# Windowed attention with routed experts on one core: value products round the column tiles, smaller value loads, split exps, and a planner that counts transfers

## The chip, the cores and the metric

The kernel runs on 1 core of one Trainium2 chip. The metric is device time in microseconds (us) of one execution, over several runs. The profile is of one more execution, whose own time is given beside its span (first to last recorded instruction).

## The reference, cut to what matters

Eight sequences of 576 tokens go through attention with 8 heads of 64. Heads 0 to 3 ("plain") see the last 32 positions, heads 4 to 7 ("dilated") the last 32 positions at distance 4. The result, as 512 features a token, goes through a mixture-of-experts step in which the 128 best-scored tokens of each sequence get a two-layer network added.

```python
scores = scale * np.matmul(q, k.transpose(0, 1, 3, 2))          # B, H = 8, 8; S, D = 576, 64
mask_plain = (rel >= 0) & (rel < 32)                            # heads 0 to 3
mask_dil = (rel >= 0) & (rel < 128) & (rel % 4 == 0)            # heads 4 to 7
attn = softmax(np.where(masks, scores, -1e9))                   # 1e-9 added to the sum
x = np.matmul(attn, v)                                          # then (B, S, 512)
scores = np.einsum('bsd,d->bs', x, w_gate)
top_idx = np.argpartition(-scores[b], 128)[:128]
h = np.maximum(x[b, top_idx] @ w1, 0.0)                         # w1: 512 x 1024, w2: 1024 x 512
out[b, top_idx] = x[b, top_idx] + sigmoid(scores[b, top_idx])[:, None] * (h @ w2)
```

## The kernel before

**Units.** Each sequence ("batch") is cut into five units, `UNITS`: plain tokens 0 to 255 and 256 to 511 (`p0`, `p1`), the last 64 tokens of both head kinds (`l0`), and the dilated queries in two halves (`d0`, `d1`). A unit g goes through `scores` (TensorE, 16 products into four column tiles of 32, line 239), `maximum` and `subtract` (VectorE), `transposes` (TensorE, line 274), `weights` (exps on ScalarE into a weight tile `pts`, line 288), `attend` (value products on TensorE, line 305), `normalise` and `divide` (VectorE, or ScalarE with eight small copies, line 334), `store` (DMAs on SP's queue) and `gate` (VectorE).

**Value products.** `attend` forms up to 16 products a unit, for four query blocks y and four heads h. Block y writes the column tile y % 2 (output partitions 0 to 63 or 64 to 127). y is the outer loop, so four products in a row go to one column tile. In the records each float32 product is two matmuls, 32 in all (24 for `l0`). A query block of 64 is two groups of 32, each with its own 64 keys of a 96-key stretch. The tile holds both groups' keys, 128 rows, with the other group's entries zero; so the values are loaded with 32 keys doubled.

**Experts.** After a batch's fifth unit come `order`, `total`, `spread`, `gather_scores`, `rank`, `mark`, `pick`, `number` and `fetch` (an indirect DMA on GpSimd that reads the stored output rows), then `experts`: transposes (`turn_x`, tile px), `ffn1` (tile ph, line 512), `relu`, `turn` and `ffn2` (tile py, line 533). The weights come in sixteen pieces through four `raw` buffers; ScalarE makes a rounded copy of each (`round_weights`, line 384), GpSimd the rest (`rest_weights`, line 388).

**Order.** Every engine runs its instructions in the order in which they are written, and a list planner, `Planner.run`, writes it. Each step has an engine, a planned cost, dependencies, a due time and buffers that it takes and frees; of the steps that can start within 0.05 us of the earliest on an engine, the one with the smallest due time comes first. Unit g is due from `unit` x g. The steps of the experts are due `route` + `ffn` = 21 us after the batch's last unit and later. Loads are steps of SP too: those of batch 0 stand ahead of the plan, later ones take 0.1 to 0.4 us and land a fixed lag later (weights 5 us):

```python
o = A("SP", 0.1, lambda i=i: load_weights(i), (), d, takes=[("raw", i)], lag=5.0)
o = A("ACT", 0.62, lambda i=i: round_weights(i), [o], d + 6)
q_in = {(0, 0): A("SP", 0.1, lambda: None, (), 0, lag=7.0), (0, 1): A("SP", 0.1, lambda: None, (), 0, lag=14.0)}
```

There is one buffer for q and k of each kind, two for the values, one for transposed scores (`t`), one for value sums (`a`) and three weight tiles, used in turn.

Of the kernel before, what the change touches and what calls it, by code (L numbers as in the profile page):

```python
# [8 lines left out]
F32 = mybir.dt.float32  # L9
# [10 lines left out]
P = 128  # L20
W = 32
DIL = 4
SR = S // DIL
G = 32
# [15 lines left out]
    unit=3.5,  # L40
# [4 lines left out]
    w1=6.0, w2=20.0, each=1.2,  # L45
    xv=2,
)


class Work:  # L50


    __slots__ = ("eng", "cost", "fn", "deps", "due", "mode", "takes", "frees", "end", "left", "users", "lag", "n")

    def __init__(self, eng, cost, fn, deps, due, mode, takes, frees, lag):
        self.eng, self.cost, self.fn, self.deps, self.due = eng, cost, fn, deps, due
        self.mode, self.takes, self.frees, self.lag = mode, takes, frees, lag
        self.end = None


class Planner:
# [3 lines left out]
    SWITCH = 0.12  # L65

    def __init__(self, bufs, switch):
        self.ops, self.bufs, self.penalty = [], bufs, switch

    def add(self, eng, cost, fn, deps=(), due=0.0, mode=None, takes=(), frees=(), lag=0.0):  # L70
        w = Work(eng, cost, fn, [d for d in deps if d is not None], due, mode, list(takes), list(frees), lag)
        w.n = len(self.ops)
        self.ops.append(w)
        return w

    def run(self):
        users, left = {}, {}
# [4 lines left out]
        free = {}  # L82
        mode = None
        ready = {}
        pools = {t: [[0.0] * n, 0, {}] for t, n in self.bufs.items()}

        order = []

        def put(w):
            t = max([d.end + d.lag + (self.HOP if d.eng != w.eng else 0.0) for d in w.deps], default=0.0)  # L90
            ready.setdefault(w.eng, []).append((t, w))

        for w in self.ops:
            if not left[w.n]:
                put(w)
        n = len(self.ops)
        while n:
            best = None
            for eng, ws in ready.items():
                now = free.get(eng, 0.0)  # L100
                cands = []
                for t, w in ws:
                    t = max(t, now)
                    ok = True
                    for tag, _ in w.takes:
                        bufs, i, _ = pools[tag]
                        if bufs[i] is None:
                            ok = False
                            break
                        t = max(t, bufs[i] + (self.HOP if bufs[i] else 0.0))  # L110
                    if ok:
                        cands.append((t, w))
# [3 lines left out]
                t, w = min(((t, w) for t, w in cands if t <= first + 0.05),  # L116
# [11 lines left out]
            w.end = t + cost  # L128
# [10 lines left out]
            order.append((t, w))  # L139
# [4 lines left out]
            n -= 1  # L144
# [4 lines left out]
def tile_window_attention_moe(ctx, tc, qt, kt, va, vb, w_gate, w1, w2, masks, mask_l, ident, slots, toks, outs, capacity):  # L149
# [8 lines left out]
    pl = Planner(BUFS, T["switch"])  # L158
# [15 lines left out]
    vp = [cp.tile([P, 9, VW], F32, name=f"vp{i}") for i in range(2)]  # L174
    vd = [cp.tile([P, 2, 4, VW], F32, name=f"vd{i}") for i in range(2)]
    vl = [cp.tile([P, 2, VW], F32, name=f"vl{i}") for i in range(2)]
    pts = [cp.tile([P, 4, 4, 2, G], F32, name=f"pt{i}") for i in range(3)]
# [20 lines left out]
    def load_vp(b, lo=0, hi=9):  # L198
        nc.sync.dma_start(out=vp[b % 2][:, lo:hi].rearrange("k c f -> k (c f)"), in_=va[b, :, (4 + lo) * VW:(4 + hi) * VW])

    def load_vd(b):
        for j in range(4):
            n = GK if j else G
            nc.sync.dma_start(out=vd[b % 2][GK * (j % 2):GK * (j % 2) + n, j // 2].rearrange("k r f -> k (r f)"),  # L204
                              in_=va[b, G * (3 - j):G * (3 - j) + n, 0:4 * VW])
# [498 lines left out]
    for t, w in pl.run():  # L704
        w.fn()
# [78 lines left out]
```

## Time and profile before

| | |
|---|---|
| median of 3 runs | 316.21 us (314.96 to 317.17) |
| profiled execution: time, span | 317.03 us, 314.4 us |
| TensorE busy | 264.9 us (84%), 3241 matmuls |
| VectorE, ScalarE, GpSimd busy | 209.1 us (67%), 132.1 us (42%), 50.1 us (16%) |
| DMA | 56.34 MB, mean 179 GB/s |

Shares are means over the whole span, and the stages differ; so the table tells how much work each engine has, and not who bounds what. Matmuls overlap in the records, and one record's duration is longer than the distance to the next. The chain of work that ended last is merged: one line is a run of instructions of the same kind.

### The profile page before, as it was taken

To read this page: it belongs to the slowest core of one execution; us is meant where nothing else is said; L and a number is where in the kernel's file an instruction comes from. 1 tells how busy PE (TensorE), PEld (TensorE's weight loads), DVE (VectorE), ACT (ScalarE), POOL (GpSimd) and SP (SyncE) were. 2 spreads that over 40 slices of the span, in tenths; PEclk is the share of its full clock that TensorE was granted. 3 is DMA by queue.
4 is the path that set the end of the run, shared out by engine and by line. 5 is a ranking of instruction groups with operands and counts; after the bars stand their busy time and mean duration, and the time that the engine had idled before them with its cause. 6 is when DMAs were issued, how large, how long until landed. Compare 5 with 4: busy or idle time off the path is not lost.

```text
span 314.4 us, 8768 instructions
## 1 busy us (share of the span) xinstructions
PE 264.9 (84%) x3241; PEld 209.5 (67%) x3241; DVE 209.1 (67%) x1184; ACT 132.1 (42%) x402; POOL 50.1 (16%) x61
## 2 busy tenths in 40 slices
PE   6404666739699999999999999998999998989993
PEld 3303555628477887787787777776887877776672
DVE  2400953865887698987978959978789838566310
ACT  1008323737244556434546445544455554413130
POOL 8609421531010002001010001010011000111101
PEclk9999975985969999999999999999999999999997
DMA  6995999799678784876999696698521312220100
GB/s 190 286 277 166 331 256 296 227 275 251 165 242 212 192 245 169 223 185 175 329 231 267 208 228 176 176 267 216 159 79 43 69 50 70 67 70 28 39 0 33
DMA packets 28363, 56.34 MB, mean 179 GB/s; under 512 B 4129, under 2 KB 14625, under 8 KB 27425
## 3 DMA queue, kind: packets, MB, share of 16 engines
q1 hardware_dynamic: 26608, 51.49, 60.2%
q0 software_dynamic: 1280, 4.20, 4.2%
q8 instruction: 25, 0.41, 0.6%
q10 hardware_dynamic: 432, 0.11, 0.2%
q14 instruction: 18, 0.14, 0.1%
HBM read 44.24 MB, written 11.53 MB: 177 GB/s over the span
## 4 chain that ended last, share of the span: by engine, by line
PE 40%; issue 32%; DMA 19%; SPq 3%; DVE 2%; POOL 2%; ACT 1%; POOLq 1%
PE a L305 11%; DMA ks<-in_kt_dram 9%; PE s L239 8%; PE ph L512 6%; PE py L533 6%; DMA vd<-in_va_dram 5%; PE t L274 4%; DMA vp<-in_va_dram 4%; PE pg L398 2%; DMA raw<-in_w_dram 2%; POOL xe L461 1%; DVE ms L253 1%; PE pa L412 1%; PE pht L521 1%; SPq L204 1%
## 5 line engine op out<-in xcount | busy, mean ns | idle before, releaser
L288 ACT ACTIVATE pt<-t 64x256 f32<-64x256 f32 (+1 forms) x160 | 58.8, 368 | 45.4 <-PE t L274 27.1
L239 PE MATMUL s<-ks,qs 128*32 128x128 f32 x1216 | 47.5, 299 | 7.2 <-DMA ks<-in_kt_dram 3.6
L253 DVE CUSTOM_DVE_ANT_0 ms<-s,mk 128x64 f32<-128x64 f32 (+1 forms) x288 | 44.4, 217 | 12.0 <-PE s L239 9.4
L239 PEld LDWEIGHTS s<-ks,qs 128*32 128x32 f32 x1216 | 37.3, 120 | 16.5 <-issue 9.2
L274 PE MATMUL t<-id,ms 128*128 128x128 f32 (+1 forms) x160 | 27.5, 294 | 22.7 <-ACT pt L288 22.7
L334 ACT ACTIVATE x<-a,rin 128x64 f32<-128x64 f32 (+1 forms) x160 | 34.8, 327 | 25.7 <-PE a L305 9.0
L274 PEld LDWEIGHTS t<-id,ms 128*128 128x128 f32 (+1 forms) x160 | 20.0, 149 | 30.3 <-ACT pt L288 23.9
L364 DVE CUSTOM_DVE_ANT_0 junk<-x,wg 128x256 bf16<-128x256 f32 x80 | 35.4, 443 | 2.3
L318 DVE TENSOR_SCALAR den<-a 128x8 f32<-128x8 f32 (+2 forms) x48 | 6.9, 158 | 39.5 <-PE a L305 37.7
L305 PE MATMUL a<-vp,pt 128*64 128x65 f32 x576 | 32.5, 238 | 0.5 <-issue 0.5
L305 PEld LDWEIGHTS a<-vp,pt 128*64 128x64 f32 x576 | 29.2, 147 | 5.2 <-issue 4.1
L428 DVE SCALAR_TENSOR_TENSOR junk<-sb,sc,thr_sb 128x576 bf16<-128x576 f32 (+1 forms) x40 | 32.4, 811 | 0.2 <-ACT sb L420 0.2
L512 PE MATMUL ph<-w1h,xh 128*128 128x512 f32 x64 | 29.6, 463 | 2.5 <-ACT sb L419 0.9
L305 PEld LDWEIGHTS a<-vd,pt 128*64 128x64 f32 x512 | 23.5, 142 | 11.1 <-issue 7.7
L305 PE MATMUL a<-vd,pt 128*64 128x65 f32 x512 | 25.7, 233 | 6.0 <-ACT pt L288 3.8
L263 DVE TENSOR_TENSOR ms<-ms,mx 128x512 f32<-128x512 f32 (+2 forms) x48 | 30.2, 641 | 0.5
L533 PE MATMUL py<-w2h,hh 128*128 128x512 f32 x64 | 29.2, 457 | 0.3 <-ACT hh L467 0.3
L461 POOL DMA_INDIRECT xe<-out_dram,ix x8 | 7.9, 989 | 128.1 <-DMA vl<-in_vb_dram 53.8
L253 DVE DVE_READ_ACCUMULATOR2_ANT mx<- 128x1 f32 (+1 forms) x320 | 25.8, 81 | 0.0
L512 PE MATMUL ph<-w1h,xl 128*128 128x512 f32 x64 | 25.4, 397 | 0.0
L533 PE MATMUL py<-w2h,hl 128*128 128x512 f32 x64 | 25.4, 396 | 0.0
L533 PE MATMUL py<-w2l,hh 128*128 128x512 f32 x64 | 25.1, 393 | 0.0
(77 smaller groups left out, 356.8 us busy)
## 6 DMA issues: line engine op xcount, KB each, us to landing
qs<-in_qt_dram SPq DMA_DIRECT2D x15, 576.0 KB
ks<-in_kt_dram SPq DMA_DIRECT2D x30, 288.0 KB
vp<-in_va_dram SPq DMA_DIRECT2D x7, 1170.0 KB
vd<-in_va_dram SPq DMA_DIRECT2D x24, 260.0 KB
raw<-in_w_dram SPq DMA_DIRECT2D x16, 256.0 KB
out_dram<-x SPq DMA_DIRECT2D x16, 256.0 KB
out_dram<-x SPq DMA_DIRECT2D x32, 128.0 KB
vl<-in_vb_dram SPq DMA_DIRECT2D x16, 97.5 KB
```

Source lines behind the costliest of these rows:

```text
L239: nc.tensor.matmul(st[G * w:G * (w + 1), c, p], q[:, p, q0:q0 + G], k[:, p, :, k0:k0 + GK], start=True, stop=True)
L253: nc.vector.tensor_tensor_reduce(out=ms[:rows, c, p, h], in0=st[:rows, c, p, h], in1=m[:rows], scale=1.0, scalar=-3.0e38, op0=ALU.add, op1 ...
L263: nc.vector.tensor_tensor(out=v, in0=v, in1=mx[:n, lo:hi].rearrange("q c p h -> q (c p h)").unsqueeze(2) .to_broadcast([n, 4 * (hi - lo), ...
L274: nc.tensor.transpose(tt[:, p, c, :rows], dt[:rows, c, p].rearrange("q h k -> q (h k)"), id32[:rows, :rows])
L288: nc.scalar.activation(pts[g % 3][GK * u:GK * (u + 1), 2 * h:2 * h + 2, 0:n, u], src, AF.Exp, scale=SCALE)
L305: nc.tensor.matmul(at[HB * (y % 2):HB * (y % 2 + 1), y // 2, f], pts[g % 3][:, h, y].rearrange("k u q -> k (u q)"), v[:, f], start=True, s ...
L334: nc.scalar.activation(x[:n, c, h, :], av[:n, c, h, 0:D], AF.Copy, scale=rin[:n, c, h:h + 1])
L364: nc.vector.tensor_tensor_reduce(out=junk[:n], in0=x[:n, c].rearrange("q h d -> q (h d)"), in1=wg[:n, 256 * dil:256 * (dil + 1)], scale=UP ...
L428: nc.vector.scalar_tensor_tensor(out=junk[:n], in0=st["sb"][:n], scalar=st["sc"][:n, t:t + 1], in1=thr_sb[:n, o:o + S], op0=ALU.subtract, ...
L461: nc.gpsimd.indirect_dma_start(out=xe[:m], out_offset=None, in_=outs[b][:, :], in_offset=bass.IndirectOffsetOnAxis(ap=ix[:m, 0:1], axis=0))
L512: nc.tensor.matmul(e["ph", n], x[:, i, :], w[:, i, n * 512:(n + 1) * 512], start=i == 0 and j == 0, stop=i == 3 and j == 2)
L533: nc.tensor.matmul(e["py"], x[:, i, :], w[:, i, :], start=i == 0 and j == 0, stop=i == 7 and j == 2)
```

## The change

`attend` goes through the query blocks in pairs, so that neighbouring products write different column tiles. `weights` writes each key once into 96 rows, where the groups share the middle keys: for units p0, p1 and d1 the second group's exps become two of 32 partitions (`PLACES`), so the unit has six exps instead of four. Four weight tiles are given out by unit (`held`) instead of three in turn. The values are loaded without doubled keys: `load_vp` 96 rows of 8 blocks in two DMAs, `load_vd` one DMA of 128 rows, `load_vl` with a third piece for the last plain keys. d1's column tiles change places, so the stores of dilated units go out in four DMAs of 32 partitions instead of two of 64.

In the planner all loads and stores have 0.6 us of SP for each DMA, a size, and land after the bytes before them at 290 GB/s, at the least 2 us later. `after` keeps a load back until 6 us before its due time. Loads of batch 0 are steps of the plan. Unit spacing is 4.5 instead of 3.5, weights are due from 10 and 24 us, the casts have due time 0, several costs are larger, and VectorE divides in the first ten units.

```diff
-    unit=3.5,
+    unit=4.5,
-    w1=6.0, w2=20.0, each=1.2,
+    w1=10.0, w2=24.0, each=0.9,
+    first=5.0, early=12.0, lead=6.0,
+    zeros=13.0,
     xv=2,
+    xe=10,
...
+            w.start, w.end = t, t + cost
+            if w.size is not None:
+                moved = max(moved, t + 1.0) + w.size / self.RATE / 1000
+                w.lag = max(w.lag, self.LAND, moved - w.end + 0.5)
...
+    def load_vp(b, lo=0, hi=8):
+        for k, src in ((slice(0, GK), slice(0, GK)), (slice(GK, 3 * G), slice(3 * G, P))):
+            nc.sync.dma_start(out=vp[b % 2][k, lo:hi].rearrange("k c f -> k (c f)"),
+                              in_=va[b, src, (4 + lo) * VW:(4 + hi) * VW])
     def load_vd(b):
+        nc.sync.dma_start(out=vd[b % 2].rearrange("k r f -> k (r f)"), in_=va[b, :, 0:4 * VW])
...
-        j = 2 * s + c
+        j = 3 - c if s else c
...
+    PLACES = {
+        ("p", 0): (((0, GK, 0),), ((G, G, 0), (GK, G, G))),
+        ("l", 0): (((0, GK, 0),), ((GK, GK, 0),)),
+        ("d", 0): (((3 * G, G, 0),), ((GK, GK, 0),)),
+    }
+    PLACES["p", 1] = PLACES["d", 1] = PLACES["p", 0]
+
+    def held(g):
+        b, u = divmod(g, NU)
+        return pts[{0: b % 2, 1: 1 - b % 2, 2: 2, 3: 3, 4: b % 2}[u]]
...
+                for to, size, k in PLACES[kind, s][u]:
+                    rows = slice(GK * h + k, GK * h + k + size)
...
+                    nc.scalar.activation(held(g)[to:to + size, 2 * h:2 * h + 2, 0:n, u], src, AF.Exp, scale=SCALE)
...
-        for y in range(3 if kind == "l" else 4):
+        n = 3 * G if kind == "p" or (kind, s) == ("d", 1) else P
+        for c in range(2):
             for h in range(4):
                 f = slice(h * (D + 1), (h + 1) * (D + 1))
+                for y in (2 * c, 2 * c + 1)[:1 if kind == "l" and c else 2]:
+                    v = {"d": vd[b % 2][:, y], "p": vp[b % 2][:, min(4 * s + y, 7)], "l": vl[b % 2][:, min(y, 2)]}[kind]
+                    nc.tensor.matmul(at[HB * (y % 2):HB * (y % 2 + 1), c, f],
+                                     held(g)[:n, h, y].rearrange("k u q -> k (u q)"), v[:n, f], start=True, stop=True)
...
+    def load(n, size, fn, deps=(), due=0.0, lead=99.0):
+        return A("SP", 0.6 * n, fn, deps, due, size=size, after=due - lead)
...
-            o = A("SP", 0.1, lambda i=i: load_weights(i), (), d, takes=[("raw", i)], lag=5.0)
-            o = A("ACT", 0.62, lambda i=i: round_weights(i), [o], d + 6)
+            o = A("SP", 0.6, lambda i=i: load_weights(i), (), d, takes=[("raw", i)], size=256, after=d)
+            o = A("ACT", 0.62, lambda i=i: round_weights(i), [o], 0.0)
...
+            at, lead = T["first"] + d - T["early"], T["lead"]
             for kd, last in ((0, 2), (1, 4)):
+                q = load(1, 590, lambda b=b, kd=kd: load_q(b, kd), [score[NU * (b - 1) + last]], at + 2 * kd * tau, lead)
+                k = load(2, 590, lambda b=b, kd=kd: load_k(b, kd), [score[NU * (b - 1) + last]], at + 2 * kd * tau, lead)
...
+        e = A("ACT", {"p": 2.3, "l": 1.3, "d": 2.3 if s else 1.55}[kind], lambda g=g: weights(g),
+              [t] + [att[i] for i in range(max(0, g - NU), g) if held(i) is held(g)], d + 3.8, frees=[("t", g)])
-        by_vector = g % T["xv"] == 0
+        by_vector = g % T["xv"] == 0 or g < T["xe"]
+        store_ops[g] = load({"p": 1, "l": 5, "d": 4}[kind], 120 if kind == "l" else 256, lambda g=g: store(g), [x], T["first"] + d + 9)
```

## Rows read from the trace of the kernel before

**Rows 1.** Busy time of each engine by stage, granted clock, DMA share, GB/s.

```profile
0.00:60.00 60.00, 30.51 (x453) 23.70 (x454) 25.16 (x187) 20.61 (x54) 28.61 (x41) 0.91 0.91 256
60.00:95.00 35.00, 26.05 (x394) 22.09 (x389) 25.21 (x145) 14.91 (x45) 6.63 (x5) 0.76 0.88 231
95.00:260.00 165.00, 162.79 (x2137) 128.91 (x2135) 133.37 (x780) 82.94 (x267) 10.02 (x10) 1.00 0.68 186
260.00:315.00 55.00, 45.50 (x270) 34.83 (x268) 25.35 (x75) 13.70 (x37) 4.90 (x5) 0.96 0.14 41
```

**Rows 2.** Instructions in order of time, all engines, the first 35 us.

```profile
13.58 1.12 PE L274 MATMUL t<-id,ms 128*128 128x128 f32 x4
...
23.92 2.56 ACT L384 CAST w1h<-raw 128x512 fp32r<-128x512 f32 x4 [21.62 <-DMA raw<-in_w_dram]
...
26.38 1.58 ACT L288 ACTIVATE pt<-t 64x256 f32<-64x256 f32 x4
```

**Rows 3.** Waits: engine and line, waited for, us in total, times, longest.

```profile
ACT w1h L384 <- DMA raw<-in_w_dram: 27.3, 3, 21.6
...
ACT w2h L384 <- DMA raw<-in_w_dram: 17.3, 4, 6.5
...
PE s L239 <- DMA ks<-in_kt_dram: 3.6, 3, 2.0
```

**Rows 4.** The same stages for tile a alone: value products.

```profile
0.00:95.00 95.00, 17.34 (x271) 16.11 (x272) 4.23 (x15) 6.94 (x32) 0.86 0.90 247
```

**Rows 5.** And for tile s alone: scores.

```profile
0.00:95.00 95.00, 21.81 (x488) 17.82 (x488) 17.55 (x116) 0.86 0.90 247
```

**Rows 6.** The chain that ended last: start, us, runs of TensorE.

```profile
95.24 1.60 PE ph L512 x6
96.85 1.01 PE s L239 x32
97.86 1.48 PE a L305 x32
...
110.80 1.19 PE a L305 x24
```

**Rows 7.** Single records of TensorE inside a short unit's value products.

```profile
258.81 0.22 PE L305 MATMUL a<-vp,pt 128*64 128x65 f32 x1
258.81 0.22 PE L305 MATMUL a<-vl,pt 128*64 128x65 f32 x1
258.87 0.22 PE L305 MATMUL a<-vp,pt 128*64 128x65 f32 x1
```

**Rows 8.** Groups of ScalarE by shape: busy us, mean ns, idle before.

```profile
L288 ACT ACTIVATE pt<-t 64x256 f32<-64x256 f32 x128 | 48.4, 378 | 41.9 <-PE t L274 24.2 <-PE a L305 14.3 <-issue 0.8
L334 ACT ACTIVATE x<-a,rin 128x64 f32<-128x64 f32 x144 | 31.7, 329 | 25.7 <-PE a L305 9.0 <-PE t L274 5.9 <-DMA out_dram<-x 4.6
...
L334 ACT ACTIVATE x<-a,rin 64x64 f32<-64x64 f32 x16 | 3.6, 314 | 0.0
```

**Rows 9.** DMA issues: count, KB each.

```profile
qs<-in_qt_dram SPq DMA_DIRECT2D x15, 576.0 KB
ks<-in_kt_dram SPq DMA_DIRECT2D x30, 288.0 KB
vp<-in_va_dram SPq DMA_DIRECT2D x7, 1170.0 KB
vd<-in_va_dram SPq DMA_DIRECT2D x24, 260.0 KB
...
vl<-in_vb_dram SPq DMA_DIRECT2D x16, 97.5 KB
```

**Rows 10.** TensorE in order of time, the tail.

```profile
270.03 1.52 PE L305 MATMUL a<-vd,pt 128*64 128x65 f32 x32 [0.20 <-PE ph L512]
...
286.95 0.36 PE L447 MATMUL pi<-toks_sb,oh 128*128 128x1 f16 x5
...
294.98 0.60 PE L497 MATMUL px<-id,xe 128*128 128x128 f32 x4
```

More of the change, by code (lines that the diff above doesn't have):

```diff
@@ L44, with __init__ @@
     switch=1.5,
-    w1=6.0, w2=20.0, each=1.2,
+    w1=10.0, w2=24.0, each=0.9,
+    first=5.0, early=12.0, lead=6.0,
+    zeros=13.0,
     xv=2,
+    xe=10,
 )
 class Work:
[L53 to L58, printed above, removed]
+    def __init__(self, n, eng, cost, fn, deps, due, mode, takes, frees, lag, size, after):
+        self.n, self.eng, self.cost, self.fn, self.due, self.mode = n, eng, cost, fn, due, mode
+        self.deps, self.takes, self.frees = [d for d in deps if d is not None], list(takes), list(frees)
+        self.lag, self.size, self.after, self.start, self.end = lag, size, after, None, None
 class Planner:
@@ L65, with __init__, add @@
     SWITCH = 0.12
[L67 to L72, printed above, removed]
+    RATE = 0.29
+    LAND = 2.0
+    def __init__(self, bufs, switch, free):
+        self.ops, self.bufs, self.penalty, self.free = [], bufs, switch, dict(free)
+    def add(self, eng, cost, fn, deps=(), due=0.0, mode=None, takes=(), frees=(), lag=0.0, size=None, after=0.0):
+        w = Work(len(self.ops), eng, cost, fn, deps, due, mode, takes, frees, lag, size, after)
         self.ops.append(w)
@@ L76, in run, with put @@
     def run(self):
-        users, left = {}, {}
+        users, left, ready, order = {}, {}, {}, []
+        free, mode, moved = self.free, None, 0.0
+        pools = {t: [[0.0] * n, 0, {}] for t, n in self.bufs.items()}
+        def put(w):
+            t = max([d.end + d.lag + (self.HOP if d.eng != w.eng else 0.0) for d in w.deps], default=0.0)
+            t = max(t, w.after)
+            ready.setdefault(w.eng, []).append((t, w))
         for w in self.ops:
@@ L143, in run @@
                     put(u)
-            n -= 1
         return order
@@ L664, in tile_window_attention_moe @@
-            v_in[b, "d"] = A("SP", 0.4, lambda b=b: load_vd(b), [old[1], v_in[b - 1, "d"]], d + 2, lag=5.0)
-        kds = {"p": (0,), "d": (1,), "l": (0, 1)}[kind]
-        score[g] = A("PE", 0.75 if kind == "l" else 0.98, lambda g=g: scores(g), [q_in[b, i] for i in kds], d, mode=32,
-                     takes=[("s", g)], lag=0.1)
-        m = A("DVE", 1.16, lambda g=g: maximum(g), [score[g]], d + 1, takes=[("ms", g)], frees=[("s", g)])
-        m = A("DVE", 0.64, lambda g=g: subtract(g), [m], d + 1)
```

163 lines of the change are left out of this document (67 added, 96 removed).

## The prediction

> **What bounds the kernel now.** I read the busy time by stage first [rows 1]. It shows three kernels in one. From 95 to 260 us TensorE is busy 162.79 of 165 us at full clock, while VectorE has 133.37, ScalarE 82.94 and the DMA share is 0.68: here only less TensorE work shortens anything. From 0 to 95 us TensorE has 30.51 + 26.05 = 56.56 of 95 us, part of it at a granted clock of 0.76 (a mixture of the 1.2 and 2.4 GHz levels), while DMA is at 0.91 and 0.88: a start limited by transfers and by whoever waits for them in order. From 260 us TensorE idles 9.5 us in the tail.
>
> Next I read the start in order of time [rows 2]. The first transposes start at 13.58 and take 1.12 us, so the first exps could run at 14.7. They run at 26.38, because ScalarE has four weight casts ahead of them and the first cast gets its data at 23.92. That is 11.7 us of standing with scores ready. The waits say the same in total [rows 3]: 27.3 us of ScalarE before w1 casts and 17.3 us before w2 casts. By 95 us the value products have 271 records [rows 4] of 152 per batch (four units of 32, one of 24), 8.9 units, while the scores have 488 [rows 5], 16 units.
>
> **Value products.** At full clock a unit's 32 records take 1.48 us, the short unit's 24 take 1.19; the scores' 32 records, each about twice as long but going round four column tiles, take 1.01 [rows 6]. Where records of the two column tiles meet by chance, both start at 258.81 and again at 258.87 [rows 7]: each tile steps by 60 ns and the two run side by side. The change makes this the order throughout: 16 records per tile at about 57 to 60 ns, some 0.93 us, and 0.07 us to drain. I take 1.0 us, with ends 0.9 (steps alone) and 1.48 (no gain). The short unit keeps 16 records in one tile, so 1.0 instead of 1.19. Contracting over 96 instead of 128 rows changes neither records nor columns: nothing. Saved: 0.48 and 0.19 us a unit. After 95 us there remain 25 long and 6 short units: 25 x 0.48 + 6 x 0.19 = 13.1 us, in a stage that TensorE bounds. The other nine lie in the start, where data come later than TensorE.
>
> The Trainium skill, TensorEngine Tiling (Array Packing), Theoretical Speedup and Key Properties, says that column tiles load weights and multiply independently, up to 2x for two tiles. By that 1.48 would become 0.74 and the sum 25 x 0.74 + 6 x 0.6 = 22 us. The rows speak against the full factor: some records of both tiles overlap already.
>
> **Exps.** An exp of 64 x 256 takes 378 ns; of two ScalarE copies, 128 and 64 partitions take 329 and 314 [rows 8]: half the partitions cost the same. Three units in five go from 4 exps to 6, so 2 x 0.38 x 3 = 2.3 us per batch. ScalarE has 82.94 of 165 us, so this hides, as does the 0.8 us later attend behind the other units in flight. Without that cover (the single transposed-score buffer held while TensorE has nothing else) it is 0.8 us x 24 units = 18 us. I take 1. The weight tile reused two units later instead of three hides behind one unit of TensorE work; uncovered, an exp waits for one attend, 1.0 us x 8.
>
> **Loads.** Per batch q and k stay at 2 x 576 + 4 x 288 = 2304 KB; values go from 1170 + 3 x 260 + 130 (half a piece, by the code) + 2 x 97.5 = 2275 KB [rows 9] to 780 + 520 + 325 = 1625. So 4.69 MB become 4.02. In the steady stage the 0.68 share hides it; in the start at 256 GB/s it is 2.6 us a batch. SP issues 12 loads and 15 stores a batch instead of 13 and 11, three more. A store waits on SP for its division, and the next batch's loads stand behind it, for which the next scores wait. What that costs now shows as TensorE's direct waits on k data, 3.6 us in three cases [rows 3]. I take 1 us for issues and waits together, and 10 as the far end, as if each of the eight batches had one such wait of 1.2.
>
> **The new order.** Transfers now have a rate in the plan, weights are due from 10 and 24 us, and casts carry due time 0 but become ready only when the plan thinks that they landed. Behind 4.35 MB (batch 0, gate and slots) the first weight lands near 19 us on the chip; the plan, at 290 GB/s, puts it at about 18. By then exps of units 0 and 1 have gone ahead. So the 11.7 us stand should go. What is late next is data: kind 1 of q and k and the values of batch 0 land by 17 to 18 us instead of the later values at 20 and more. A unit then needs its scores, VectorE, transposes, exps and attend, about 7 us, so batch 0 is through by 27 us. Then w1 (2.1 MB), batch 1 (4.0) and stores (0.9) bring the sum to 11.4 MB, 45 us at 256 GB/s; batch 1 is through by 52.
>
> Routing and fetching of batch 0 take what the tail shows for the last one: attend at 270.03 to pick at 286.95 [rows 10] is 17 us, and I add an estimated 4 for the fetch. The first expert matmul comes near 48. What before had done by 95 us is 8.9 x 1.48 + 16 x 1.01 + about 8 for transposes and routing (an estimate) = 37 us of TensorE work, 33 with the new products. The changed kernel has done batches 0 and 1 (24.6: five units of scores, transposes and products at 2.5 each), routing (2) and 4 to 6 us of expert work by about 57 us. **X = 57** takes the place of 95. Bounds: 46 if nothing but the chain counts, 75 if half of the old losses stay (late w2 casts, half clock). The zeros on GpSimd grow by one weight tile of three clears and lose two value clears; they stay ahead of the data and cost nothing.
>
> The Trainium skill, DMA: Bandwidth & Descriptors, Measured, gives 341 GB/s for a 1 MB transfer. By it 11.4 MB come in 33 us and X falls to about 47. The row decides: 256 GB/s at a share of 0.91 [rows 1].
>
> **Tail.** Unit spacing 4.5 puts expert pieces nearer to their batch (15 + 6 over 4.5 is 4.7 units instead of 6), so fewer pieces are left to fill the last batch's routing. Between the last attend at 270.03 and the last px at 294.98 are 25 us [rows 10], all but filled; from the end of that attend routing and fetch need about 20. I expect 10 to 12 us of filler, so the tail idles 3 us more while it starts earlier. Bounds -3 and 9.
>
> **Sum.** 314.4 - 95.2 (the first expert matmul [rows 6]) = 219.2. Less 13.1 is 206.1; plus tail 3, exps 1, queue 1, and 1 for VectorE, which rises to 133.37 / 153 = 87% of the shortened stage: 212. With X 57, a span of 269. The division by VectorE in the first two batches lies in the transfer-bound start: nothing; beside a busy VectorE, 5 x 0.7 (the plan's cost) = 3.5 us. The profiled execution took 317.03, 2.6 more than its span; 269 + 2.6 = 272. The median of the runs, 316.2, is 0.8 under the profiled one, so **271 us**. The case's own ends: 46 + 206 + 1.8 = 254, and 75 + 206 + 9 + 5 + 1.8 = 297; the far ends of exps and queue at the middle X give 57 + 206 + 3 + 18 + 10 + 1 + 1.8 = 297 too.
>
> **Rivals.** (a) The columns don't overlap better, TensorE issuing as now: X about 61 and no 13.1, so 61 + 219 + 6 + 1.8 = 288. For it: the weight loads may be what steps. Against: rows 7. (b) The start doesn't shorten: DMA was at 0.91, and in-order stalls only change places. X = 95: 95 + 212 + 1.8 = 309; with X at 85, 299. For it: 15.4 MB moved in 60 us, no more than 14% of the load bytes go. Against: 3 batches of scores had their data by 95, with nine units attended; data was not what the exps lacked. (c) Slower: casts with due 0 go ahead of exps wherever the plan believes the weights landed. If that takes in the w2 casts ahead of batch 0's exps, ScalarE stands until w2 has landed, 4.35 + 4.2 + 4.0 + 0.9 MB, 53 us, not 26.4: X = 95 + 27, span 122 + 212, and 336 us. It decides if more than half of that stand, 14 us beyond today's, is real. Against: w2's due is 24 and the four raw buffers admit four weights until GpSimd frees one. (d) VectorE becomes the bound after 95 us: 133.4 us of work plus stalls holds the stage near 160 instead of 153, giving 278, inside the forecast.
>
> **How the numbers follow.** Forecast 0.72 (d included), (a) 0.07, (b) 0.13, (c) 0.05, under 254 0.03. The range 253 to 300 takes the forecast whole, (a), and the better third of (b): 0.83. A change within 1%, about what three runs from 314.96 to 317.17 can tell, needs a start that costs 13 us more just to cancel the products: 0.03. Slower by over 1%: 0.05. Faster: 0.92.
>
> **What would show it.** The unit's 32 value records in 0.95 to 1.05 us at full clock; the first exps before 17 us; the first expert matmul before 55; ScalarE's waits on raw weights under 15 us in total; TensorE busy over 95% from 70 us to the last attend. It is wrong if the products stay at 1.48, if exps again stand behind casts, or if SP's stores hold back q and k so that scores wait for data in each batch.

## The result and the profile after

The changed kernel takes 300.65 us (median of 4 runs, 299.25 to 302.35) where the kernel before takes 315.77 on the same chip: ratio 0.9519, 95% interval 0.9457 to 0.9581. A second measurement on another chip (after_again below) gave 299.42 and 0.9349, 0.923 to 0.9468. The forecast was 271 us with a range of 253 to 300: the sign was right, the gain of 15 us (20 on the other chip) less than half of the forecast 45. Runs of one kernel scatter upwards by some per cent, so medians here take all runs, while the ratios compare only runs near the fastest of their kernel. The profiled execution took 299.25 us, with a span of 297.5.

First the stages of the changed kernel, as [rows 1] show them before (busy us of TensorE, its weight loads, VectorE, ScalarE, GpSimd; then granted clock, DMA share, GB/s); the last attend now ends at 257 instead of 272.

```profile
0.00:60.00 60.00, 41.27 (x639) 32.72 (x640) 39.25 (x235) 23.03 (x57) 24.56 (x38) 0.77 0.90 235
60.00:95.00 35.00, 25.10 (x370) 19.93 (x371) 28.84 (x147) 16.40 (x42) 11.48 (x9) 0.76 0.94 262
95.00:257.00 162.00, 157.99 (x2098) 122.40 (x2087) 134.25 (x764) 93.22 (x291) 11.38 (x11) 0.98 0.59 161
257.00:298.00 41.00, 31.39 (x150) 23.52 (x149) 15.45 (x45) 8.44 (x22) 4.11 (x4) 0.96 0.13 43
```

TensorE is busy 66.37 of the first 95 us instead of 56.56. How much more work that is, its records tell: the value products (tile a), the scores (s) and the first layer of the experts (ph) in the first 95 us, beside [rows 4] and [rows 5].

```profile
0.00:95.00 95.00, 19.35 (x368) 16.80 (x368) 9.76 (x27) 1.74 (x8) 0.77 0.92 245
0.00:95.00 95.00, 21.09 (x515) 17.47 (x519) 18.81 (x123) 0.77 0.92 245
0.00:95.00 95.00, 7.87 (x24) 4.63 (x24) 1.24 (x2) 0.77 0.92 245
```

That is 368 value records instead of 271 (three units more), 515 score records instead of 488, and batch 0's whole first layer instead of nothing. At the full-clock durations of [rows 6] this is some 12 us of TensorE work (an estimate: 97 x 1.48 / 32 + 27 x 1.01 / 32 + 24 x 1.60 / 6). So the start, which was to give back 38 us, gave back some 12. After 95 us TensorE's busy time falls from 162.79 + 45.50 = 208.3 us [rows 1] to 157.99 + 31.39 = 189.4, through these 12 us and the cheaper products, and its idle time to the end of the span rises from 11.1 to 13.1. That is the whole 16.9 us between the two spans. The DMA share is what it was, 0.90 and 0.94 against 0.91 and 0.88, and so are the bytes: 60 x 235 + 35 x 262 = 23.3 MB now, 23.4 before.

Next the start in order of time, all engines, beside [rows 2], and TensorE's first expert matmul.

```profile
12.84 1.12 PE L271 MATMUL t<-id,ms 128*128 128x128 f32 x4
...
14.00 2.38 ACT L299 ACTIVATE pt<-t 64x256 f32<-64x256 f32 x6 [11.70 <-PE t L271]
```

```profile
81.89 0.80 PE L520 MATMUL ph<-w1h,xh 128*128 128x512 f32 x1
```

ScalarE now waits for the transposes, and the exps start at 14.00 instead of 26.38. But the first expert matmul comes at 81.9, not at 57. ScalarE's waits for weights, beside [rows 3] (us in total, times, longest):

```profile
ACT w2h L393 <- DMA raw<-in_w_dram: 8.5, 4, 3.6
...
ACT w1h L393 <- DMA raw<-in_w_dram: 2.0, 2, 1.0
```

The chain that ended last (start, us, what), with runs that answer to [rows 6]:

```profile
51.52 8.44 DMA raw<-in_w_dram
...
91.04 1.08 PE a L313 x32
...
96.75 1.07 PE a L313 x24
```

A unit's products go from 1.48 to 1.08 us, the short unit's from 1.19 to 1.07. The first line is a piece of w2 on the way to batch 0's routing. Its cause is in SP's queue, read in order of time:

```profile
39.70 1.28 SPq L358 DMA_DIRECT2D out_dram<-x  x1
41.03 1.97 SPq L360 DMA_DIRECT2D out_dram<-x  x4
43.09 3.21 SPq L355 DMA_DIRECT2D out_dram<-x  x4
46.35 0.58 SPq L200 DMA_DIRECT2D vd<-in_va_dram  x1
47.03 2.49 SPq L355 DMA_DIRECT2D out_dram<-x  x4
49.62 0.53 SPq L183 DMA_DIRECT2D qs<-in_qt_dram  x1
50.20 1.22 SPq L190 DMA_DIRECT2D ks<-in_kt_dram  x2
51.52 0.54 SPq L385 DMA_DIRECT2D raw<-in_w_dram  x1
```

Thirteen stores of batch 0 go out between 39.7 and 49.5 us, with the next loads behind them.

The tail on TensorE, beside [rows 10]:

```profile
255.85 1.15 PE L313 MATMUL a<-vd,pt 96*64 96x65 f32 x32
...
273.79 0.36 PE L455 MATMUL pi<-toks_sb,oh 128*128 128x1 f16 x5
...
278.16 0.63 PE L505 MATMUL px<-id,xe 128*128 128x128 f32 x4 [1.71 <-DMA xe<-out_dram,ix]
```

Attend to pick is 17.9 us, as it was (16.9). From the end of the last attend to the end of the span, TensorE idles 9.1 of 40.5 us, before 7.8 of 42.9.

### The profile page after: what moved, and what is told of

Its sections match the earlier page's. It is cut to its first block, busy times and chain, and to the rows that moved or that the text cites. A ratio compares the mean times of both kernels' runs of the same rounds, so it can differ in the third digit from the quotient of the medians.

```text
span 297.5 us, 8808 instructions
## 1 busy us (share of the span) xinstructions
PE 255.8 (86%) x3241; PEld 198.6 (67%) x3241; DVE 217.8 (73%) x1190; ACT 141.1 (47%) x410; POOL 51.5 (17%) x62
## 4 chain that ended last, share of the span: by engine, by line
PE 57%; DVE 14%; issue 12%; DMA 10%; SPq 4%; ACT 1%; POOLq 0%; POOL 0%; DVEq 0%; ACTq 0%
PE ph L520 15%; PE py L541 11%; PE a L313 10%; PE s L236 9%; PE t L271 5%; DMA xe<-out_dram,ix 4%; DVE ms L250 3%; DMA ks<-in_kt_dram 3%; DMA raw<-in_w_dram 3%; PE pht L529 2%; DVE junk L373 2%; SPq L355 2%; DVE ms L260 2%; DVE junk L436 2%; PE pg L406 2%
## 5 line engine op out<-in xcount | busy, mean ns | idle before, releaser
L299 ACT ACTIVATE pt<-t 32x256 f32<-32x256 f32 (+2 forms) x208 | 76.7, 369 | 64.0 <-PE t L271 55.8
L250 DVE CUSTOM_DVE_ANT_0 ms<-s,mk 128x64 f32<-128x64 f32 (+1 forms) x288 | 44.3, 216 | 11.4 <-PE s L236 9.4
L373 DVE CUSTOM_DVE_ANT_0 junk<-x,wg 128x256 bf16<-128x256 f32 x80 | 38.5, 481 | 1.9
L436 DVE SCALAR_TENSOR_TENSOR junk<-sb,sc,thr_sb 128x576 bf16<-128x576 f32 (+1 forms) x40 | 33.8, 845 | 6.4 <-ACT sb L428 6.2
L342 ACT ACTIVATE x<-a,rin 128x64 f32<-128x64 f32 (+1 forms) x120 | 26.1, 329 | 23.3 <-PE a L313 11.1
L271 PE MATMUL t<-id,ms 128*128 128x128 f32 (+1 forms) x160 | 27.5, 294 | 5.5 <-DVE den L326 5.5
L520 PE MATMUL ph<-w1h,xh 128*128 128x512 f32 x64 | 30.6, 478 | 1.5 <-ACT xh L475 1.4
L313 PE MATMUL a<-vd,pt 96*64 96x65 f32 (+1 forms) x512 | 21.6, 242 | 5.3 <-DVE x L336 4.3
L520 PE MATMUL ph<-w1l,xh 128*128 128x512 f32 x64 | 25.9, 404 | 0.0
L313 PEld LDWEIGHTS a<-vd,pt 96*64 96x64 f32 (+1 forms) x512 | 19.0, 153 | 9.8 <-issue 6.3
L313 PEld LDWEIGHTS a<-vp,pt 96*64 96x64 f32 x512 | 18.1, 148 | 9.8 <-ACT pt L299 4.6
L313 PE MATMUL a<-vp,pt 96*64 96x65 f32 x512 | 20.8, 237 | 4.0 <-ACT pt L299 2.2
```

Source lines behind the costliest of these rows:

```text
L250: nc.vector.tensor_tensor_reduce(out=ms[:rows, c, p, h], in0=st[:rows, c, p, h], in1=m[:rows], scale=1.0, scalar=-3.0e38, op0=ALU.add, op1 ...
L271: nc.tensor.transpose(tt[:, p, c, :rows], dt[:rows, c, p].rearrange("q h k -> q (h k)"), id32[:rows, :rows])
L299: nc.scalar.activation(held(g)[to:to + size, 2 * h:2 * h + 2, 0:n, u], src, AF.Exp, scale=SCALE)
L313: nc.tensor.matmul(at[HB * (y % 2):HB * (y % 2 + 1), c, f], held(g)[:n, h, y].rearrange("k u q -> k (u q)"), v[:n, f], start=True, stop=True)
L342: nc.scalar.activation(x[:n, c, h, :], av[:n, c, h, 0:D], AF.Copy, scale=rin[:n, c, h:h + 1])
L373: nc.vector.tensor_tensor_reduce(out=junk[:n], in0=x[:n, c].rearrange("q h d -> q (h d)"), in1=wg[:n, 256 * dil:256 * (dil + 1)], scale=UP ...
```

## The experiments

Ratios are to the kernel before on the same chip, with 95% intervals; "against the changed kernel" means against 0.9519 and 0.9349, its two measurements. "First expert matmul" is the start of the first record of tile ph. Where only a few per cent divide two kernels of different chips, the two measurements' own distance is to be kept in mind.

**The parts of the change, alone and taken out.** products_only puts the new loop order into the kernel before:

```diff
-        for y in range(3 if kind == "l" else 4):
+        for c in range(2):
             for h in range(4):
+                for y in (2 * c, 2 * c + 1)[:1 if kind == "l" and c else 2]:
```

> The kernel before with nothing changed but the loop order of the value products (the two column tiles alternate). Theory: the products are worth 0.40 us a long unit and 0.12 a short one after the start, some 12 us, whatever the plan does: 303 to 305 us. Rival: the changed kernel's whole gain came from its start, and faster products only turn into waits: within 3 us of before.

311.13 us (304.84 to 314.57) beside 317.13, with no interval: about 6 us less by the medians, between the theory and the rival; the fastest run alone, 304.84, would mean some 11. Its stages (columns as above) and its largest wait of TensorE (22.7 us before):

```profile
0.00:60.00 60.00, 30.16 (x437) 23.12 (x439) 25.31 (x186) 19.91 (x52) 28.48 (x41) 0.69 0.90 255
60.00:95.00 35.00, 21.95 (x372) 18.14 (x372) 24.15 (x139) 15.66 (x47) 6.63 (x5) 0.79 0.88 225
```

```profile
PE t L274 <- ACT pt L288: 22.9, 5, 13.2
```

The same transfers in the same time; in this profile what the products save there becomes idle time (52.11 busy instead of 56.56), with 240 value records done instead of 271. The first expert matmul comes at 97.6, 2.4 us later than before. The profiled execution took 310.94 us, and its mean clock was 0.90, against 0.955 in the one of 304.84; that the lower clock of its start comes from the products isn't shown.

after_old_products is the reverse, the changed kernel with the old loop order:

```diff
-            for h in range(4):
-                f = slice(h * (D + 1), (h + 1) * (D + 1))
-                for y in (2 * c, 2 * c + 1)[:1 if kind == "l" and c else 2]:
+            for y in (2 * c, 2 * c + 1)[:1 if kind == "l" and c else 2]:
+                for h in range(4):
+                    f = slice(h * (D + 1), (h + 1) * (D + 1))
```

> The changed kernel with the old loop order of the value products. Theory: 12 us slower than the changed kernel, near 312 us, so that what the plan, the exps and the loads bring together is only some 3 us. Rival (the start brought the 15 us): 301 to 303 us.

306.61 us (302.95 to 310.57), 0.9674 (0.9454 to 0.9893): some 6 us more than the changed kernel's 300.65 by the medians, 2 to 5 by its two fastest runs (302.95 and 305.41), and the intervals overlap. So the products are worth about 6 us in either kernel by the medians, and the runs don't fix that better than 2 to 11.

planner_only gives the kernel before the new planner with its numbers (cut below); all_but_planner is the reverse, the changed kernel with the old planner:

```diff
-    unit=3.5,
+    unit=4.5,
...
+    RATE = 0.29
+    LAND = 2.0
```

> The changed planner, its load steps and constants, with the old products, exps, weight tiles, loads and stores (their sizes and numbers of DMAs given to the plan). Theory: the start gains what the trace shows, 13 us to the first expert matmul, less what more exps and stores took there, so 300 to 306 us if these were the harm, and 312 to 316 us if the plan itself spends the start on the wrong things. Rival: no difference to before, 314 to 318 us.

> The new products, exps, weight tiles, loads and stores under the old planner and its constants (the exps' cost alone is the new one). Theory: the products' 12 us less 1 to 3 for longer exps and more store DMAs in the start: 305 to 308 us. Rival (the planner is what counts): 313 to 317 us.

planner_only 325.19 us, 1.0302 (1.0117 to 1.0486), slower, and beyond all that was expected of it; all_but_planner 318.24 (310.09 to 327.16 over ten runs), 0.9974 (0.9913 to 1.0035), near its rival. Neither part alone gives a clear gain, together they give 15 us. But each of these two also plans another order from other costs, so the next two hold the order instead: old_order_new_work runs the changed steps in the order of before, new_order_old_work the old steps in the order of after. Each cut below is against the kernel whose steps it runs.

```diff
 # old_order_new_work: planner, costs and due times of before
-    unit=4.5,
+    unit=3.5,
 # new_order_old_work: those of after
-    unit=3.5,
+    unit=4.5,
```

> Exactly the order of instruction groups of the kernel before, on every engine, with the new products, exps, weight tiles, loads and stores (the plan is given the old costs, so it writes the old order). Theory: with the order held, the parts add up: products 6 us, 650 KB a batch 8 us, less 2 for exps: 303 to 307 us. Rival (the new work gains only with its own plan): 314 to 319 us, as in the all-but-planner run.

> Exactly the order of the changed kernel on every engine, with the old products, exps, weight tiles, loads and stores. Theory: the changed kernel plus 6 for products, 8 for bytes, less 2 for exps: 310 to 314 us, so the new order by itself is worth 3 to 6 us against before. Rival (the new order is worse by itself, as in the planner-only run): 320 us and more.

In both, some weight tiles are written before the products of an earlier unit have read them, so part of the rows get another unit's weights; instructions and sizes are those named. 313.25 us, 0.9812 (0.9676 to 0.9947), where 303 to 307 was expected if the parts add up, and 313.85, 0.9892 (0.9776 to 1.0009), within the expected 310 to 314. The work alone gives 2%, the order alone perhaps 1%; together they give 5 to 6.5%. The losses of planner_only and all_but_planner went with their own orders.

The traces show why the halves add up to less than the whole. From 95 us to the end, old_order_new_work, then new_order_old_work:

```profile
95.00:311.60 216.60, 200.59 (x2406) 154.86 (x2402) 158.12 (x843) 107.19 (x332) 15.18 (x15) 0.99 0.51 135
95.00:311.50 216.50, 198.64 (x2226) 155.47 (x2225) 150.26 (x797) 88.45 (x278) 15.52 (x15) 0.98 0.50 142
```

Against the 208.3 busy and 11.1 idle us of before, the work alone leaves TensorE 7.7 us less to do and 4.9 more to wait, the order alone 9.7 less and 6.8 more. Both together leave it 18.9 less and 2.0 more (in the second profile of the changed kernel, after_again, 22.1 less and 6.5 more). The savings in work add up; the idle time doesn't. The start's gain comes with the order: by 95 us new_order_old_work has done 368 value records and the 24 of the first layer, with its first expert matmul at 80.1, while old_order_new_work stands where before stood, with 272 and none, though it moved 21.9 MB by then instead of 23.4.

split_exps_before cuts the second group's exps in two in the kernel before, for the same units:

```diff
+                cut = u and not (kind == "l" or (kind, s) == ("d", 0))
+                for z in ((0, 1) if cut else (0,)):
+                    e = G if cut else GK
+                    nc.scalar.activation(pts[g % 3][GK * u + G * z:GK * u + G * z + e, 2 * h:2 * h + 2, 0:n, u], src[G * z:G * z + e], ...)
```

> The kernel before with nothing changed but the second group's exps of units p0, p1 and d1 in two pieces of 32 partitions each, same result, same plan: six exps instead of four. Theory: hidden, as predicted, 1 us or under 0.5%. Rival (ScalarE's chain of transposes, exps and products sets the pace): 5 us slower or more, as much as the all-but-planner run lost to the products-only run.

319.62 us, 1.0107 (1.0033 to 1.0181): 3.4 us by the ratio, 1 to 6, where the forecast had 1.

more_bytes gives the changed kernel back its load bytes, 650 KB a batch that nothing reads, in the same order; they come in two more DMAs a batch on SP:

```diff
+        for t in again:
+            nc.sync.dma_start(out=t.rearrange("k r f -> k (r f)"), in_=va[b, 0:t.shape[0], 0:4 * VW])
```

> The changed kernel with 650 KB more to load in each batch, into rows that nobody reads, in the same order and unknown to the plan: as many bytes as the kernel before loaded. Theory: transfers bind only before 95 us; 2.6 us a batch for three batches, 4 to 8 us slower. Rival (data were not what the start lacked): within 2 us.

308.72 us, 0.9776 (0.9671 to 0.9881), about 8 more than the changed kernel. The stages 60 to 82 and 82 to 120 us of it, and of the changed kernel, with the latter stage of after_again last:

```profile
60.00:82.00 22.00, 10.22 (x186) 7.96 (x190) 17.43 (x73) 8.78 (x21) 6.57 (x6) 0.69 0.89 253
82.00:120.00 38.00, 31.59 (x424) 24.53 (x414) 28.34 (x162) 18.27 (x53) 7.32 (x6) 0.93 0.97 250
```

```profile
60.00:82.00 22.00, 12.10 (x202) 9.37 (x199) 19.70 (x77) 9.99 (x23) 8.59 (x7) 0.65 0.89 266
82.00:120.00 38.00, 38.00 (x500) 29.82 (x501) 32.52 (x208) 23.08 (x71) 5.06 (x5) 0.98 0.86 229
82.00:120.00 38.00, 33.85 (x458) 26.64 (x457) 31.13 (x196) 21.39 (x66) 4.42 (x4) 1.00 0.90 212
```

The first expert matmul is at 82.6 instead of 81.9, so the loss comes behind it: from 82 to 120 us DMA is at 0.97, and TensorE has 31.59 of 38 us. The busy time of this stage differs by itself from one profile of the changed kernel to the other (38.00 and 33.85), but the work done doesn't: by 120 us more_bytes has 444 value records and 24 of the first layer, the changed kernel 488 and 44, after_again 488 and 41. Transfers hold back more than the stage that I took as the start. How much of the 8 us is bytes and how much the two more DMAs isn't separated.

**The chain of batch 0.** In the plan a unit's gate waits for its store, because both hold the same buffer; batch 0's routing starts at 54.6, 16 us behind its last attend. gates_free lets the store alone hold the buffer:

```diff
-        x = xs.pop(g)
+        x = xs[g]
...
-        gates[g] = A("DVE", 0.86, lambda g=g: gate(g), [x, store_ops[g], gate_in], d + 9, frees=[("x", g)])
+        gates[g] = A("DVE", 0.86, lambda g=g: gate(g), [x, gate_in], d + 9)
+        A("end", 0.0, lambda g=g: xs.pop(g), [gates[g], store_ops[g]], 0.0, frees=[("x", g)])
```

> The changed kernel, but in the plan the gate dots of a unit need only the divided rows, and no longer the landing of the unit's store, which the plan's transfer count puts up to 10 us behind prefetched loads; the row buffer is given back by a step after both. Theory (routing comes late because gates stand behind stores in the order): order of batch 0 follows its last attend by under 8 us instead of 16, the first expert matmul comes at 68 to 73 us, and the time falls by 6 to 10 us, to 291 to 295. Rival (VectorE and TensorE have no room before 80 us anyway): first expert matmul after 78, time within 3 us.

299.09 us, 0.9379 (0.929 to 0.9467), beside after_again's 299.42 on the same chip. Batch 0's first routing matmul and first expert matmul in it, on TensorE, and its longest wait:

```profile
41.75 1.27 PE L406 MATMUL pg<-sd,perm 128*128 128x2 f32 x8 [0.83 <-DVE sd L373]
...
68.49 0.50 PE L520 MATMUL ph<-w1h,xh 128*128 128x512 f32 x1
```

```profile
PE px L505 <- DMA xe<-out_dram,ix: 9.3, 4, 2.7
```

The routing starts 13 us sooner (41.8 against 54.6) and the first expert matmul comes 13 us sooner (68.5), as the theory said; the time, which it put at 291 to 295, doesn't change. The lead was real and was lost again: by 95 us gates_free has as many value records as the changed kernel (368) and 21 records of the experts' second layer, where the changed kernel has none; by 140 us both have 48 of these, and gates_free has a unit less attended (544 value records against 576). From 95 to 140 us TensorE is busy 38.5 of 45 us in gates_free, 43.2 and 40.9 in the two profiles of the changed kernel.

w2_late makes the w2 loads due at 45 us, rate_measured plans with 240 GB/s, about what the trace shows, two_t gives the transposed scores a second buffer and takes it from the three of the experts' tiles, unit_4_4 moves the unit spacing by a little, and no_rest makes GpSimd's part of the weights a ScalarE copy of zeros, so the low parts of the weights are left out:

```diff
-    w1=10.0, w2=24.0, each=0.9,
+    w1=10.0, w2=45.0, each=0.9,
 # rate_measured
-    RATE = 0.29
+    RATE = 0.24
 # two_t
-    BUFS = dict(s=2, t=1, a=1, m=3, ...)
+    BUFS = dict(s=2, t=2, a=1, m=2, ...)
 # unit_4_4
-    unit=4.5,
+    unit=4.4,
 # no_rest
-        nc.gpsimd.tensor_tensor(out=lo, in0=raw.pop(i), in1=hi.bitcast(F32), op=ALU.subtract)
+        nc.scalar.activation(lo, raw.pop(i), AF.Copy, scale=0.0)
...
-            weight_ops[i] = A("POOL", 1.3, lambda i=i: rest_weights(i), [o], 0.0, frees=[("raw", i)])
+            weight_ops[i] = A("ACT", 0.62, lambda i=i: rest_weights(i), [o], 0.0, frees=[("raw", i)])
```

> The changed kernel with the w2 weights due from 45 instead of 24 us. Theory of the gates: batch 0's order does not move, only the 3.6 us in which the copy of routing scores stood behind a w2 cast go: first expert matmul at 76 to 80 us, time 298 to 302. Rival (casts on ScalarE hold the start, as they did before): first expert matmul before 73 and time under 296.

> The changed kernel with a planned transfer rate of 240 GB/s, which is what the trace shows for the first 95 us (245), instead of 290. Theory (the plan runs ahead of the chip, so orders written by it stand): TensorE idles less after 95 us, under 3 us until the last attend, and the time falls by 2 to 6 us. Rival: any other order is worse, as the late w2 weights showed, 303 to 318 us, because the loads are then placed so that the plan itself starves.

> The changed kernel with two banks for transposed scores instead of one and two instead of three for the experts' tiles. Theory: in the first 60 us a unit takes 4 us because transposes, exps and products of successive units share one bank in turn; with two, batch 0 is attended by 33 us instead of 39 and TensorE idles 5 us less before 95 us. What the experts lose to the missing bank is not known, so the time may go either way by 5. Rival (the single bank is not what holds the start): batch 0 attended at 37 to 40 us, as before this edit.

> The changed kernel with units due every 4.4 instead of 4.5 us: no instruction added or removed, but 205 of TensorE's 296 steps stand at another place in the order. Theory (the order that the list planner happens on is worth up to 10 us either way): 304 to 312 us. Rival (the order is stable, and only its start counts): 298 to 302 us.

> The changed kernel without GpSimd's subtraction of the rounded weights: the low parts are set to zero on ScalarE instead, 0.62 us each, so GpSimd is free of tensor work in the start; the low parts of the weights are left out of the result. Theory: VectorE instructions no longer stretch by a microsecond while GpSimd subtracts, VectorE's first 95 us shrink by 6 to 10 us of busy time, but the first expert matmul moves by under 4 us and the time by under 4. Rival (this sharing is what held batch 0's units): first expert matmul before 75 us, time under 296.

> The changed kernel once more, as the measure for the next three on the same chip: 299 to 303 us, and the first expert matmul at 80 to 84 us in the profile.

| | us | ratio, 95% interval | first expert matmul, us |
|---|---|---|---|
| after_again | 299.42 | 0.9349, 0.923 to 0.9468 | 80.2 |
| w2_late | 318.43 | 0.998, 0.9932 to 1.0028 | 80.7 |
| rate_measured | 312.79 | 0.9857, 0.976 to 0.9955 | 77.3 |
| two_t | 325.45 | 1.0298, 1.0217 to 1.0379 | 78.5 |
| unit_4_4 | 303.12 | 0.9546, 0.9435 to 0.9657 | 78.1 |
| no_rest | 300.91 | 0.9364, 0.924 to 0.9488 | 77.6 |

None of these beats the changed kernel, and three lose 12 to 26 us though their first expert matmul comes at much the same time or earlier; w2_late and two_t lose more than was expected of them. Telling the plan the true rate made it worse, as the rival said. Nudging the unit spacing reorders 205 of 296 steps of TensorE and costs nothing clear, so the gain doesn't hang on one single order, though these three lose it. no_rest frees VectorE of GpSimd's company and gains nothing.

Where the three lose can be read. By 95 us they have done as much as the changed kernel (392, 424 and 424 value records in w2_late, two_t and rate_measured, and the first layer). From there to the end TensorE idles 29.8, 30.1 and 27.5 us, against 13.1 in the changed kernel and 17.6 in after_again. The largest of these waits is, in each, that of px for the fetched rows (11.1, 7.8 and 6.8 us, against 3.6 and 6.1), but it is only a part. So orders that differ little in the start differ behind it.

**SP's stores.** stores_doubled sends the dilated stores in eight DMAs of 16 partitions instead of four of 32, fewer_stores sends those of the first dilated unit in two of 64, and stores_by_gpsimd issues the dilated stores on GpSimd. The order written out is the same in all three.

```diff
 # stores_doubled
+                    for z in range(0, G, 16):
+                        nc.sync.dma_start(out=o[P * j:P * (j + 1), 256:512].rearrange("(n c r) f -> r n c f", c=2, r=2)[r, z:z + 16],
+                                          in_=x[i + z:i + z + 16])
 # fewer_stores, s == 0
+                    nc.sync.dma_start(out=o[0:2 * P, 256:512].rearrange("(n c r) f -> r n c f", c=2, r=2)[r],
+                                      in_=x[HB * r:HB * (r + 1)])
 # stores_by_gpsimd
-                    nc.sync.dma_start(out=o[P * j:P * (j + 1), 256:512]...
+                    nc.gpsimd.dma_start(out=o[P * j:P * (j + 1), 256:512]...
```

> The changed kernel with each store of dilated units in 16 instead of 32 partitions, so twice as many, eight more DMAs a batch on SP, in the same order. Theory: SP has room after 95 us, and in the start the queue of stores is on the way of the loads behind it: 1 to 3 us slower. Rival (the issue of stores is what holds the start): 6 us slower or more, first expert matmul after 86 us.

> The changed kernel with the first dilated unit of a batch stored by two DMAs of 64 partitions instead of four of 32 (its column tiles did not change places); the order written out is the same, two DMAs fewer a batch on SP. Theory that the issue of stores on SP costs (eight more a batch cost some 12 us): 2 to 4 us faster than the changed kernel, near 297. Theory that only many small transfers hurt, or that the doubled run showed something else: no difference, 300 to 301.

> The changed kernel with the dilated units' stores issued on GpSimd instead of SP: eight store DMAs a batch leave SP's queue, nothing else moves in the order written out. Theory that stores on SP hold back the loads behind them: the next batch's q and k and the w2 weights are issued some 5 us earlier in the start, and the time falls by 4 to 10 us, 290 to 296. Rival: GpSimd stands before each store until its division is done, with the second steps of the weights behind it, and issues as slowly: the wait only changes its engine, 300 to 315.

stores_doubled: 312.49 us, 0.9875 (0.9778 to 0.9971), some 12 us more than the changed kernel, as its rival said, though the first expert matmul stays at 82.3. Its stages 60 to 82 and 82 to 120 us:

```profile
60.00:82.00 22.00, 10.02 (x192) 8.10 (x195) 17.29 (x71) 8.74 (x21) 6.39 (x5) 0.69 0.81 223
82.00:120.00 38.00, 34.56 (x388) 26.40 (x382) 28.30 (x157) 18.45 (x55) 7.50 (x6) 0.83 0.91 232
```

DMA moves 223 instead of 266 GB/s from 60 to 82 us, at a share of 0.81 instead of 0.89: the DMA engines stand idle more, which points to the queue and not to the transfers. fewer_stores: 296.85 us (294.67 to 297.49), 0.9377 (0.9327 to 0.9427), the lowest median of all, but its ratio lies between the changed kernel's two, so it may be 2% faster or nothing. stores_by_gpsimd: 301.51 us, 0.9523 (0.9451 to 0.9595), no gain. The Trainium skill, DMA: Bandwidth & Descriptors, Rules for kernel authors, says that spreading DMAs over issuing engines brings no bandwidth and saves only sequencer issue time; the 301.51 agrees, and what issue time it took off SP brought nothing either. Doubling the stores costs; that the change's own four more a batch cost anything isn't shown.

## Why the prediction was wrong

**The step that failed is "X = 57 takes the place of 95".** X, the first expert matmul, came at 81.9, outside its bounds of 46 to 75. That is 25 us of the 28.5 us between the forecast span of 269 and the 297.5; the rest, from X to the end, is 297.5 - 81.9 = 215.6 against the forecast 212. Three parts of the step were wrong.

*Batch 0 through by 27 us:* its last attend ends at 38.8. The first unit kept to the forecast 7 us, with k landed at 10.8 and its attend ended at 18.0. The other four, which the step had overlap, followed one at a time, at 24.5, 27.6, 34.3 and 38.8; from 20.95 to 32.01 the chain that ended last stands on VectorE without a break. Neither the clock nor GpSimd's share in this is large: in after_again, with a granted clock of 0.87 instead of 0.77 over the first 60 us, batch 0 was through at 39.6, and in no_rest, without GpSimd's subtractions, at 37.5. With a second buffer for transposed scores (two_t) it was 36.4.

*Routing and fetching in 21 us,* taken from the tail: it took 43, from 38.8 to 81.9. The plan has the gate wait for a store that stands on SP behind loads fetched ahead, so the routing starts at 54.6; then it stands on ScalarE behind a w2 cast (59.98) whose data were issued behind thirteen stores; ranking and marking last until 69.8; and px (77.04) and the first expert matmul stand on TensorE behind later units' transposes, scores and products. The fetch itself landed 4.1 us after its issue, as the estimated 4 had it.

*X as the lever.* This is the deeper fault. The sum took the work done by X and called the rest saved. gates_free moved X by 13 us with no effect, and w2_late, two_t and rate_measured have an X of 77.3 to 80.7 and end 12 to 26 us later: they wait it away after 95 us. I had counted the 11.4 MB that X alone needs; the queue had moved 243 GB/s x 81.9 us = 19.9 MB by X, since what later units need goes in between. That transfers alone bound the start isn't shown: its bytes were the same before and after (23.4 and 23.3 MB in 95 us, at a DMA share near 0.9), but new_order_old_work moved 25.6 MB in the same time, at a share of 0.95, for the same work done.

Rival (b), "the start doesn't shorten: DMA was at 0.91, and in-order stalls only change places", with 299 us at X = 85, is near what came: X 82 and 300.65. The start did shorten, by some 12 us of work and not by 38. I had put (b) at 0.13 because nine units were attended where three batches of scores had their data. That was so, and the change did attend more of them (11 units by 81.9); but the exps, freed from the casts, met other waits.

**The other terms.** *Products:* right in mechanism, 1.08 us instead of 1.0, so a saving of 0.40 and 0.12 a unit. 25 x 0.40 + 6 x 0.12 = 10.7 us instead of 13.1; the full factor of two (0.74) is refuted by the 1.08. No row shows the 0.07 us to drain; a tile's 16 records took 1.08 in all. What the saving was worth by the runs is less still, about 6 us: in products_only TensorE idles 42.9 us of the first 95 instead of 38.4 and is a unit behind. *Loads:* 2.6 us a batch for three batches agrees with the 8 us of more_bytes, but these came after 82 us, and two more DMAs a batch are in them. *Exps:* 3.4 us instead of 1, inside the bounds. *Stores and SP:* 1 us for three more issues may have been too little, with doubled stores at 12 us for eight; but two fewer (fewer_stores) gave nothing clear, and what the change's own cost stays open. *Tail:* it idles 1.3 us more (9.1 against 7.8) instead of 3.

**The named checks.** Products at 0.95 to 1.05: just missed. First exps before 17: met, 14.0. First expert matmul before 55: missed by 27 us. ScalarE's waits for raw weights under 15 us: met, 10.5. TensorE over 95% busy from 70 us: missed until 82 (12.10 of 22 us from 60 on), then met: 157.99 of 162. Scores waiting for k in each batch: no, 4.7 us in two cases, both before 95 us (3.6 in three before). VectorE is no bound, with 134.25 of 162, so rival (d) falls; (a) falls with the 1.08; (c), casts ahead of exps, with the exps at 14.0.

**How the 15 us come about.** Taken out of the changed kernel one at a time, the products cost about 6 us, the fewer bytes about 8, and the old order 13 (old_order_new_work). These don't add up to a sum: put into the old order, products, bytes and exps together gave 3 us, and the order alone 3, because most of the work that either saved came back as idle time after 95 us. Together 18.9 us of work were saved and 2.0 came back. What stays open is why one order leaves TensorE these waits and another doesn't; neither the first expert matmul nor the plan's rate says which is good.

## What to carry to other kernels

Before a chain in a transfer-bound start is priced at a saving, count the bytes that go by its end in the trace, not only those that it needs itself; here the first expert matmul moved by 13 us and not by 38. A milestone such as the first expert matmul is a forecast of the time only if the other work done by then is held fixed, and if the lead isn't waited away later. Compare kernels by the records done at a given time, and by the work and the idle time of the bounding engine after it: the work that two changes save adds up, the idle time doesn't. Work taken from an engine that starves in one stage comes back there as idle time, so count only the units of the stage that it bounds.

## What the runs showed of the hardware

**VectorE beside GpSimd.** In the changed kernel's start, and later:

```profile
27.23 2.94 POOL L397 TENSOR_TENSOR w1l<-raw,w1h 128x512 fp32r<-128x512 f32 x2 [1.08 <-ACT w1h L393]
27.25 1.80 DVE L260 TENSOR_TENSOR ms<-ms,mx 128x512 f32<-128x512 f32 x1
28.98 1.48 DVE L373 CUSTOM_DVE_ANT_0 junk<-x,wg 128x256 bf16<-128x256 f32 x1
...
30.50 0.42 DVE L373 CUSTOM_DVE_ANT_0 junk<-x,wg 128x256 bf16<-128x256 f32 x1
...
73.34 0.69 DVE L260 TENSOR_TENSOR ms<-ms,mx 128x512 f32<-128x512 f32 x1
```

The subtraction takes 1.80 us while GpSimd subtracts and 0.69 alone, the gate 1.48 and 0.42: each about 1.1 us more. The Trainium skill, SBUF — State Buffer, SBUF: two separate sides, says that a VectorE operation with two inputs from SBUF and a GpSimd operation that reads SBUF lock each other out for a whole instruction; these rows agree. In no_rest VectorE's busy time over 0 to 95 us falls from 39.25 + 28.84 = 68.1 to 63.8 us, and the time stays.

**The clock of an engine that starves.** From 60 to 82 us TensorE was busy 12.10 of 22 us and the granted clock was 0.65, mostly the 1.2 GHz level; from 82 to 120, busy throughout, 0.98. The same 32 records of scores, at a granted clock of 0.50 and of 1.00:

```profile
80.02 1.94 PE L236 MATMUL s<-ks,qs 128*32 128x128 f32 x32
...
86.04 1.08 PE L236 MATMUL s<-ks,qs 128*32 128x128 f32 x32
```

So a busy share of the start overstates its work. The mean clock doesn't repair that: in the first 60 us the two profiles of the changed kernel have 41.27 busy us at 0.77 and 41.62 at 0.87 for nearly the same records (639 and 635). Records are the safer measure.
